# A list scheduler for the float32 items, the weight decoding and the first 20 steps of attention with two MLPs

## The chip, the cores and the metric

One core of a Trainium2 chip runs the kernel. The metric is the device time of one execution in microseconds (us). Engines: PE is TensorE, ACT is ScalarE, DVE is VectorE, POOL is GpSimd, SP is SyncE, whose queue issues the DMAs.

## The reference

Attention over a window of 128 keys for B = 4, H = 8, S = 576, D = 64, then two MLPs on the 2304 tokens of 512 features:

```python
scores = np.where(mask, scale * (q @ k.T) + bias, -1000000000.0)
attn = np.exp(scores - np.max(scores, axis=-1, keepdims=True))
attn = attn / (np.sum(attn, axis=-1, keepdims=True) + 1e-09)
x = (attn @ v).transpose(0, 2, 1, 3).reshape(2304, 512)
h = x @ w_in                                      # 512 -> 2048
x = (np.maximum(h, 0.0) + alpha * np.minimum(h, 0.0)) @ w_out
h = x @ w_in2
out = (h * (1.0 / (1.0 + np.exp(-1.702 * h)))) @ w_out2
```

The MLP weights come as float64.

## The kernel before

**Items.** An item is one head of one batch and one of two row ranges, 64 in all. The first `FP = 24` are done in float32 ahead of everything else; the others are interleaved with the later MLP steps. An item n of the first 24 goes through: `a_load` (two DMAs into one of five raw buffers: q and k at L412, v at L414), `a_qk` (PE, scores `s`), `a_bias` (DVE, L490), `a_exp` (ACT, L506), `a_sum` (POOL, an add on `st`, L521), `a_recip` (DVE, L516), `a_norm` (DVE, L537), `a_trans` (PE transposes, L552), `a_pt_hi` (ACT copies the transposed scores to `pt`, L559), `a_split_v` (POOL copies v from the raw buffer to a zero-padded `vz`, L448), `a_av` (PE, `o<-pt,vz`, L609), and after every second item `a_xf` (ACT and DVE split the result into `xh` and `xl`). `pt`, `tt` and `st` have three buffers, `vz` two. `busy(n)` puts idle matmuls between the first items. A raw buffer is loaded anew when its scores and its `vz` copy are done.

**Decoding.** The first MLP's weights are 32 chunks: chunk 2f is the `w_in` part and chunk 2f+1 the `w_out` part of block f. A chunk is loaded (`w_load`, 512 KB into one of four staging buffers `ws`), scaled twice on ACT (`w_scale`, `wd<-ws` and `ws<-ws`, L152, L155), shifted and added on DVE (`w_shift` L159, `w_add` L164), and split by `w_split` into `wh` (ACT) and `wl` (DVE), both through the helpers at L110 and L115. `wd` has three buffers.

**Steps.** Behind the items come steps (k, f). The first 32 alternate between two token blocks, k = 0, 1, with f = s // 2 for step s. `m1_h` makes h(s) with 12 matmuls (L680) from `xh`, `xl` and block f's `wh`, `wl`, in the order wh, wh, wl for each quarter; `m1_n` (ACT, L694) and `m1_g` (DVE L700, then ACT's cast `gh` L702) apply the slope of the first MLP; `m1_lo` (DVE) makes `gl`; `m1_o` adds g's product with the `w_out` part (12 matmuls, L726), `LAG = 2` steps later. PE's order is h(s), o(s-2), h(s+1), o(s-1), and so on.

**What sets the order.** All of it is written by hand. The item loop over n emits the stages of several items in a fixed pattern, a raw load for item n+4, and at the loop's steps named in `DEC` one pass of decoding. In the loop over steps each step up to s = 31 does one load (`w_ahead`), shift, add, split and scale through `w(...)`, which takes the next chunk for that stage. `chain(mark)` pins each engine's program order as written for the items; `pinned` and `held` do so for the steps. The minimum of the two halves of `relt` (a mask for later items, L1141) is written behind the items.

Of the kernel before, what the change touches and what calls it, by code (L numbers as in the profile page):

```python
# [11 lines left out]
F32 = mybir.dt.float32  # L12
# [9 lines left out]
P = 128  # L22
# [50 lines left out]
def tile_window_attention__then__two_mlps(  # L73
# [47 lines left out]
    def pin(ins):  # L121
        if pinned:
            tc.keep_in_program_order(ins)
# [22 lines left out]
        return s[:, :, 0], s[:, :, 1]  # L146

    def w_scale(i):
        lo, hi = w_words(i)
        layer, f, part = chunks[i]  # L150
        wtm[i] = wtmp.tile([P, DM], I32, tag="wd", name="wd")
        pin(nc.scalar.activation(  # L152
            wtm[i].bitcast(F32), hi.bitcast(F32), AF.Prelu, scale=2.0**-112, alpha=-(2.0**32)
        ))
        pin(nc.scalar.mul(lo, lo.bitcast(U32), 2.0**-29))  # L155

    def w_shift(i):
# [440 lines left out]
    @stage  # L598
    def a_av(n, b, u, h, U):
        if n < FP:  # L600
            if h % 2:
                x = st["x", n] = st["x", n - 1]
            else:
                i = n // 2 % 2
                x = pso.tile([P, 2, T1], F32, tag=f"o{i}", name=f"o{i}").rearrange("p i t -> p (i t)")
                st["x", n] = x
            pt, vz = pts[n % 3], vzs[n % 2]
# [488 lines left out]
    a_load(4, (0,))  # L1096
    a_load(3, (1,))
    bias_load(4, 4)
    make_identity(nc, ident)
    make_own()  # L1100
    busy(0)

    def only(fn, n, *args):
        if n < FP:
            fn(n, *args)

    for n in range(-1, FP + 4):
        only(a_qk, n + 1)
        busy(n + 2)
        only(a_bias, n)  # L1110
        only(a_xf, n - 4, 0)
        only(a_pt_hi, n - 2)
        only(a_av, n - 3)
        only(a_recip, n - 1)
        only(a_norm, n - 1, "dve")
        only(a_trans, n - 1)
        only(a_xf, n - 4, 1)
        only(a_exp, n)
        only(a_split_v, n - 1)
        only(a_sum, n)  # L1120
        if n == 0:
            a_load(4, (1,))
        elif 0 < n < FP - 4:
            a_load(n + 4)
        elif FP - 4 < n < FP - 1:
            a_load(n + 3)
        if n in (8, 10, 12, 14):
            w_load(wdone.setdefault("load", 0))
            wdone["load"] += 1
        if n == 16:  # L1130
            nc.sync.dma_start(out=relt, in_=rel)
            nc.sync.dma_start(out=alph, in_=alpha)
        if n in DEC:
            w("split")
            w("shift")
            w("add")
            w_ahead()
            w("scale")
    chain(mark)
    nc.gpsimd.tensor_scalar(beta, alph, -1.0, 1.0, op0=ALU.mult, op1=ALU.add)  # L1140
    nc.vector.tensor_tensor(relt[:, :P], relt[:, :P], relt[:, P:], op=ALU.min)  # L1141
    at0.close()
    pa.close()
    a_parts()
    pj = ExitStack()
    psa["j"] = pj.enter_context(tc.tile_pool(name="ps_j", bufs=1, space=PSUM))
    psa["a"] = pj.enter_context(tc.tile_pool(name="ps_b", bufs=2, space=PSUM))
    gp[0] = p1.enter_context(tc.tile_pool(name="g", bufs=3, side="right"))
    gt[0] = p1.enter_context(tc.tile_pool(name="gt", bufs=2, side="right"))
    xsp[0] = p1.enter_context(tc.tile_pool(name="xs", bufs=2, side="right"))  # L1150
# [316 lines left out]
```

## Time and profile before

| | us |
|---|---|
| median of 3 runs (lowest, highest) | 883.58 (882.83, 889.0) |
| the profiled execution | 884.44 |
| its span | 882.7 |
| PE busy in the span | 866.8 (98%) |
| DVE busy | 696.7 (79%) |
| ACT busy | 551.7 (62%) |
| POOL busy | 184.8 (21%) |

The items take the first 58.8 us (h(0) starts at 58.79), the 32 steps go on to about 145, and the rest of the span is later steps, the second MLP and the output. Rows of the trace are read as follows: a timeline row has its start, its length, the engine, the line, the operation, output <- inputs, and in brackets how long the engine was idle before it and what it waited for. A row of waits names the engine that waited, its instruction, and what ended the wait. The times between the starts of two rows of one engine tell what an operation costs in a row of others; its own length also has the part that overlaps.

### The profile page before, as it was taken

What the parts mean: (1) busy time and instruction counts of PE and PEld (TensorE: products, weight loads), DVE (VectorE), ACT (ScalarE), POOL (GpSimd) and SP (SyncE); (2) the same over time, 40 slices, a digit from 0 to 9 for tenths busy, and PEclk for the clock granted to TensorE, in tenths of its full rate; (3) what the DMA queues carried; (4) which work ended last, traced back from release to release, by engine and by line L of the source; (5) the groups of instructions that cost most, each with busy time, mean ns of one, the idle gap of its engine ahead of it and who ended that gap; (6) DMA issues with size and microseconds to landing.
All of it is one profiled execution on the core that took longest, in us unless ns stands there. A gap on an engine that the chain in (4) does not pass through costs nothing.

```text
span 882.7 us, 19445 instructions
## 1 busy us (share of the span) xinstructions
PE 866.8 (98%) x6804; PEld 838.2 (95%) x6804; DVE 696.7 (79%) x1763; ACT 551.7 (62%) x1397; POOL 184.8 (21%) x349
## 2 busy tenths in 40 slices
PE   9879999999999999999999999999999999999998
PEld 7769999999999999999988889999999999999997
DVE  5689887679999999999567777557575699988875
ACT  6798886677677767676455557655556754444432
POOL 3220002355666556655200000000000000000000
PEclk9999999999999999999999999999999999999999
DMA  4756662224335234242042334757678873544423
GB/s 137 198 163 212 194 193 88 89 87 149 114 88 185 77 117 133 90 141 83 1 143 96 96 106 163 225 206 241 219 261 284 294 264 112 171 140 124 152 61 96
DMA packets 74209, 132.28 MB, mean 150 GB/s; under 512 B 14336, under 2 KB 33792, under 8 KB 74112
## 3 DMA queue, kind: packets, MB, share of 16 engines
q1 hardware_dynamic: 74112, 131.05, 47.1%
q8 instruction: 53, 0.87, 0.4%
q14 instruction: 44, 0.36, 0.1%
HBM read 94.31 MB, written 36.70 MB: 148 GB/s over the span
## 4 chain that ended last, share of the span: by engine, by line
PE 60%; ACT 0%; DVE 0%; issue 0%; DVEq 0%; ACTq 0%
PE p L980 19%; PE p L883 14%; PE h L680 9%; PE h L883 6%; PE p L726 5%; PE o L726 4%; PE x L621 1%; PE s L471 1%; PE pt L545 0%; PE s L472 0%; ACT oh L110 0%; DVE ob L997 0%; ACT G L892 0%; DVE se L997 0%; DVE wd L997 0%
## 5 line engine op out<-in xcount | busy, mean ns | idle before, releaser
L680 PE MATMUL h<-xh,wh 128*128 128x256 f32 (+1 forms) x512 | 149.8, 293 | 0.4 <-DVE g L700 0.4
L680 PE MATMUL h<-xh,wl 128*128 128x256 f32 (+1 forms) x512 | 149.5, 292 | 0.0
L680 PE MATMUL h<-xl,wh 128*128 128x256 f32 (+1 forms) x512 | 149.5, 292 | 0.0
L980 PE MATMUL p<-wl,oh 128*128 128x256 f32 x504 | 136.2, 276 | 0.0
L980 PE MATMUL p<-wh,oh 128*128 128x256 f32 x504 | 135.0, 277 | 0.3 <-ACT oh L110 0.3
L980 PE MATMUL p<-wh,ol 128*128 128x256 f32 x504 | 131.0, 276 | 0.0
L726 PE MATMUL o<-gh,wh 128*128 128x256 f32 x448 | 127.6, 285 | 0.0
L726 PE MATMUL o<-gl,wh 128*128 128x256 f32 x448 | 124.0, 277 | 0.0
L726 PE MATMUL o<-gh,wl 128*128 128x256 f32 x448 | 123.8, 276 | 0.0
L680 PEld LDWEIGHTS h<-xh,wh 128*128 128x128 f32 x512 | 96.7, 189 | 3.3 <-DVE g L700 0.6
L680 PEld LDWEIGHTS h<-xh,wl 128*128 128x128 f32 x512 | 96.6, 189 | 2.9
L680 PEld LDWEIGHTS h<-xl,wh 128*128 128x128 f32 x512 | 96.7, 189 | 2.7
L1011 POOL TENSOR_TENSOR ob<-wd,se 128x256 f32<-128x256 f32 x1 | 0.7, 746 | 448.2 <-ACT se L1009 448.2
L980 PEld LDWEIGHTS p<-wl,oh 128*128 128x128 f32 x504 | 94.6, 188 | 0.0
L980 PEld LDWEIGHTS p<-wh,oh 128*128 128x128 f32 x504 | 93.7, 188 | 0.5 <-ACT oh L110 0.5
L980 PEld LDWEIGHTS p<-wh,ol 128*128 128x128 f32 x504 | 91.3, 188 | 0.0
L694 ACT ACTIVATE n<-h 128x256 f32<-128x256 f32 (+1 forms) x128 | 52.0, 406 | 53.6 <-PE h L680 52.9
L726 PEld LDWEIGHTS o<-gl,wh 128*128 128x128 f32 x448 | 84.3, 188 | 0.1
L726 PEld LDWEIGHTS o<-gh,wh 128*128 128x128 f32 x448 | 84.2, 188 | 0.1
L726 PEld LDWEIGHTS o<-gh,wl 128*128 128x128 f32 x448 | 84.1, 188 | 0.0
L702 ACT CAST gh<-g 128x256 fp32r<-128x256 f32 x112 | 45.2, 404 | 60.4 <-DVE g L700 60.2
L110 ACT CAST oh<-gs 128x1024 fp32r<-128x1024 f32 (+1 forms) x40 | 38.1, 964 | 62.9 <-issue 28.2
(182 smaller groups left out, 2460.9 us busy)
## 6 DMA issues: line engine op xcount, KB each, us to landing
g2d<-G SPq DMA_DIRECT2D x64, 288.0 KB, 3.2
ws<-in_w_in_dram SPq DMA_DIRECT2D x32, 512.0 KB, 3.7
ws<-in_w_out_dram SPq DMA_DIRECT2D x32, 512.0 KB, 4.0
gr<-g2d SPq DMA_DIRECT2D x32, 512.0 KB, 4.1
raw<-in_u_dram SPq DMA_DIRECT2D x32, 352.0 KB, 3.0
raw<-in_u_dram SPq DMA_DIRECT2D x32, 160.0 KB, 2.5
xr<-x2d SPq DMA_DIRECT2D x40, 128.0 KB, 2.6
wo2d<-wd SPq DMA_DIRECT2D x16, 256.0 KB, 2.7
```

Of the source, the lines that this page charges most:

```text
L110: return nc.scalar.copy(o, i)
L471: keep(nc.tensor.matmul(o[:, :n_], q, kh[:, ks : ks + n_], start=True, stop=False))
L621: keep(nc.tensor.matmul(x[:, oc : oc + nq], v, p[:, col : col + nq], start=(i == 0 and k == 0), stop=(i == len(js) - 1 and k == (j < 4)), ...
L680: keep(nc.tensor.matmul(ph, w[:, 0, c * P : (c + 1) * P], x[:, c, r : r + n], start=(c == 0 and i == 0), stop=(c == NC - 1 and i == 2),))
L694: nc.scalar.activation(n, ph, AF.Relu, scale=-1.0)
L702: nc.scalar.copy(gh, g)
L726: keep(nc.tensor.matmul(o, w[:, 1, c * P : (c + 1) * P], g, start=(first and (k == KM or c % 2 == 0) and i == 0), stop=(last and i == 2), ...
L883: tc.keep_in_program_order(nc.tensor.matmul(o, w[:, cc * P : (cc + 1) * P], x[:, h, cc, i, :], start=first and cc == 0 and k == 0, stop=la ...
L980: mm = nc.tensor.matmul(o[:, m, :], g[:, a, m * P : (m + 1) * P], w, start=(p == 0 and m == 0 and i == 0), stop=(p == NF // 2 - 1 and i == 2),
L1011: nc.gpsimd.tensor_tensor(c11, p1_, p2_, op=ALU.add)
```

## The change

A function `emission()` builds a list of all operations of the 24 items, of their loads, of the decoding of 32 chunks and of the steps, with their dependences, a duration for each kind and a delay between engines, and schedules them: PE has a fixed order, each other engine takes the operation that can start first, and among equals the one due first. The list is cut where o(17) starts; n, g, gh and gl of the first `SJ = 20` steps are kept, and pieces of decoding whose chunk number is below one that was done are appended. The kernel then writes its program in that order, and `chain(mark)` pins it. From step 20 on the old loop goes on. `w_scale`, `w_split` and `m1_g` are cut into pieces so that each can be placed by itself, `vz` has four buffers, and two loads of items 24 and 25 follow the list. The `min` on `relt` is written behind it (L1257 in the new file).

```diff
-DEC = (19, 21, 23, 24, 25, 26)
+SJ = 20
+XLAG = 3
...
+def emission():
+    seq = []
+    for n in range(-1, FP + XLAG + 1):
+        for k, i in (("s", n + 1), ("b", n + 2), ("x", n - XLAG), ("tr", n - 1)):
...
+            bias=(("s", i), ("tr", i - 3)), exp=(("bias", i),), add=(("exp", i),), recip=(("add", i),),
+            norm=(("recip", i),), pt=(("tr", i), ("x", i - 3)), vz=(("raw", i), ("x", i - 4)),
+            xh=(("x", i),), xl=(("xh", i),), raw=(("vz", i - 5), ("s", i - 5)),
+            ld=(("ad", i - NST), ("s", 8 + 2 * i)), sc1=(("ld", i), ("lo", i - NWD)), sc2=(("ld", i),), sh=(("sc1", i),),
+            ad=(("sh", i), ("sc2", i)), hi=(("ad", i),), lo=(("hi", i),), n=(("h", i), ("gl", i - 2), ("xl", FP - 1), ("xl", FP - 3)),
+            g=(("n", i),), gh=(("g", i), ("o", i - 3)), gl=(("gh", i),), b=(),
...
+    stop = next(t for t, _, z in out if z == ("o", SJ - 1 - LAG))
+    rows = ("n", "g", "gh", "gl")
+    out = [(t, p, z) for t, p, z in out if t <= stop or z[0] in rows and z[1] < SJ]
+    out = [x for x in out if not (x[2][0] in rows + ("h", "o") and x[2][1] >= SJ)]
+    done = {z for _, _, z in out}
+    out = sorted(out, key=lambda x: (x[0], x[1]))
+    out = [z for _, _, z in out]
+    for k in ("ld", "sc1", "sc2", "sh", "ad", "hi", "lo"):
+        last = max(i for q, i in done if q == k or {q, k} in ({"hi", "lo"}, {"sc1", "sc2"}))
+        out += [(k, i) for i in range(last + 1) if (k, i) not in done]
+    return out
...
+    vzf = [first.tile([P, 2, P], F32, name=f"vzf{i}") for i in range(2)]
+    vzs += vzf
-            nc.gpsimd.tensor_copy(vzs[n % 2][:, :, d0 : d0 + D], vr)
+            nc.gpsimd.tensor_copy(vzs[n % 4][:, :, d0 : d0 + D], vr)
...
-    for n in range(-1, FP + 4):
...
+    for k, i in emission():
+        if (k, i) == ("n", 0):
+            joint()
+        emit[k](i)
+        if (k, i) == ("raw", FP - 1):
+            nc.sync.dma_start(out=relt, in_=rel)
+            nc.sync.dma_start(out=alph, in_=alpha)
+    chain(mark)
+    pinned.append(True)
+    nc.vector.tensor_tensor(relt[:, :P], relt[:, :P], relt[:, P:], op=ALU.min)
...
+    a_load(FP)
+    a_load(FP + 1)
     for s, (k, f) in enumerate(steps):
+        if s < SJ:
+            continue
```

PE's order of operations is the same in both programs. On the other engines it moves; three places are shown, with the rows of the program in each engine's order.

**Place 1, DVE and ACT about step 21.** In the rows a `wl12` or `wh12` belongs to block 12 (steps 24 and 25); the numbers behind the underscore tell tiles apart. `h_1727` of the old program and `h_1706` of the new one are h(21). DVE before, from g(20) on:

```order
L700 SCALAR_TENSOR_TENSOR g_1701<-n_1698,beta_73,h_1683 128x256
L164 ISA wd_1668<-ws_1568,wd_1668 128x1024
L700 SCALAR_TENSOR_TENSOR g_1745<-n_1742,beta_73,h_1727 128x256
L115 TENSOR_TENSOR gl_1706<-g_1701,gh_1703 128x256
L115 TENSOR_TENSOR wl12_1709<-wd_1626,wh12_1708 128x512
L159 TENSOR_SCALAR wd_1712<-wd_1712 128x512
L164 ISA wd_1712<-ws_1610,wd_1712 128x1024
L115 TENSOR_TENSOR gl_1750<-g_1745,gh_1747 128x256
L115 TENSOR_TENSOR wl12_1709<-wd_1668,wh12_1708 128x512
```

DVE now, from g(21) on:

```order
L808 SCALAR_TENSOR_TENSOR g_1724<-n_1721,beta_73,h_1706 128x256
L262 ISA wd_1656<-ws_1603,wd_1656 128x1024
L207 TENSOR_TENSOR gl_1729<-g_1724,gh_1726 128x256
L207 TENSOR_TENSOR wl11_1732<-wd_1654,wh11_1731 128x512
L257 TENSOR_SCALAR wd_1658<-wd_1658 128x512
L808 SCALAR_TENSOR_TENSOR g_1768<-n_1765,beta_73,h_1750 128x256
L262 ISA wd_1658<-ws_1563,wd_1658 128x1024
L207 TENSOR_TENSOR gl_1773<-g_1768,gh_1770 128x256
L207 TENSOR_TENSOR wl11_1732<-wd_1656,wh11_1731 128x512
```

Behind g(21) the old program splits chunks 24 and 25 (block 12), the new one chunk 22 (block 11), which h(22) reads; the shift and add in between belong to later chunks. ACT before, from n(20) on:

```order
L694 ACTIVATE n_1698<-h_1683 128x256
L694 ACTIVATE n_1742<-h_1727 128x256
L702 CAST gh_1703<-g_1701 128x256
L110 CAST wh12_1708<-wd_1626 128x512
L152 ACTIVATE wd_1712<-ws_1610 128x512
L155 ACTIVATE ws_1610<-ws_1610 128x512
L702 CAST gh_1747<-g_1745 128x256
L110 CAST wh12_1708<-wd_1668 128x512
```

ACT now, from n(21) on:

```order
L802 ACTIVATE n_1721<-h_1706 128x256
L247 ACTIVATE wd_1658<-ws_1563 128x512
L253 ACTIVATE ws_1603<-ws_1603 128x512
L814 CAST gh_1726<-g_1724 128x256
L202 CAST wh11_1731<-wd_1654 128x512
L247 ACTIVATE wd_1691<-ws_1677 128x512
L253 ACTIVATE ws_1677<-ws_1677 128x512
L802 ACTIVATE n_1765<-h_1750 128x256
```

Both programs have two scalings between an n and a gh. In the old one the `wh` behind gh(20) is of chunk 24, in the new one the `wh` behind gh(21) is of chunk 22.

**Place 2, POOL at the first items.** `st` is the add behind the exponentials of items 0, 1, 2; `vz` and `vzf` are the copies of v. Before:

```order
L521 TENSOR_SCALAR st0_133<-st0_133 128x2
L448 COPY vz0_152<-raw0_131 128x2x64
L521 TENSOR_SCALAR st1_134<-st1_134 128x2
L448 COPY vz1_153<-raw1_132 128x2x64
L521 TENSOR_SCALAR st2_135<-st2_135 128x2
L448 COPY vz0_152<-rawf0_122 128x2x64
```

Now:

```order
L556 COPY vz0_154<-raw0_133 128x2x64
L556 COPY vz1_155<-raw1_134 128x2x64
L556 COPY vzf0_125<-rawf0_122 128x2x64
L556 COPY vzf1_126<-rawf1_123 128x2x64
L629 TENSOR_SCALAR st0_135<-st0_135 128x2
L629 TENSOR_SCALAR st1_136<-st1_136 128x2
```

Adds and copies alternated; now four copies stand ahead of the first add. On DVE in the same place the three passes of item 2's bias moved ahead of item 0's reciprocal.

**Place 3, DVE about step 27.** `g_1995` before and `g_1984` now are g(27); `q` belongs to item 24, `wl14` and `wd_1821` to chunk 28, which h(28) reads. Before:

```order
L700 SCALAR_TENSOR_TENSOR g_1995<-n_1993,beta_73,h_1980 128x256
L115 TENSOR_TENSOR gl_1962<-g_1957,gh_1959 128x256
L115 TENSOR_TENSOR wl15_1965<-wd_1882,wh15_1964 128x512
L115 TENSOR_TENSOR gl_1999<-g_1995,gh_1997 128x256
L115 TENSOR_TENSOR wl15_1965<-wd_1922,wh15_1964 128x512
L700 SCALAR_TENSOR_TENSOR g_2035<-n_2033,beta_73,h_2015 128x256
```

Now:

```order
L808 SCALAR_TENSOR_TENSOR g_1984<-n_1981,beta_73,h_1968 128x256
L262 ISA wd_1863<-ws_1849,wd_1863 128x1024
L544 SCALAR_TENSOR_TENSOR q_145<-raw0_133,q_145 64x256
L257 TENSOR_SCALAR wd_1821<-wd_1821 128x512
L207 TENSOR_TENSOR gl_1989<-g_1984,gh_1986 128x256
L262 ISA wd_1821<-ws_1805,wd_1821 128x1024
L207 TENSOR_TENSOR wl14_1992<-wd_1821,wh14_1991 128x512
```

The old program splits the last two chunks, 30 and 31, about g(27); the new one adds and splits chunk 28 there, and the add stands behind that of chunk 29, the `q` and gl.

## Rows read from the trace of the kernel before

**Rows 1.** Busy time by stretch: from:to, length, busy us (count) per engine, clock.
```profile
52.50:57.50 5.00, 2.31 (x13) 1.70 (x12) 4.30 (x11) 4.58 (x11) 0.68 (x2) 1.00 0.47 153
57.50:62.50 5.00, 4.87 (x26) 4.72 (x27) 3.93 (x9) 4.09 (x8) 0.58 (x6) 0.66 0.74 211
70.00:110.00 40.00, 40.00 (x355) 40.00 (x355) 36.20 (x76) 33.77 (x75) 0.00 (x0) 1.00 0.66 199
```

**Rows 2.** Waits of PE, 0 to 66 us: total, times, longest.
```profile
PE pt L552 <- DVE ttf L537: 3.0, 3, 2.0
PE s L462 <- DMA rawf<-in_u_dram: 1.7, 2, 0.8
...
PE pt L552 <- DVE tt L537: 1.1, 2, 0.8
PE s L462 <- DMA raw<-in_u_dram: 0.8, 1, 0.8
PE o L609 <- ACT ptf L559: 0.8, 1, 0.8
PE h L680 <- DVE g L700: 0.4, 1, 0.4
```

**Rows 3.** Waits of SyncE's queue, 0 to 60 us: total, times, longest.
```profile
SPq L414 <- POOL st L521: 13.3, 14, 2.3
```

**Rows 4.** Timeline, 41 to 42.6 us: start, length, engine, line, operation, [idle before <- releaser].
```profile
41.63 0.29 DVE L1141 TENSOR_TENSOR relt<-relt 128x128 f32<-128x128 f32 x1 [2.06 <-DMA relt<-in_rel_dram]
...
42.27 0.50 PE L552 MATMUL pt<-ident,ttf 128*128 128x128 f32 x2 [0.77 <-DVE ttf L537]
```

**Rows 5.** Timeline, 6.9 to 10 us.
```profile
6.99 0.58 SPq L414 DMA_DIRECT2D rawf<-in_u_dram  x1
...
8.11 0.22 POOL L521 TENSOR_SCALAR st<-st 128x2 f32<-128x2 f32 x1 [3.56 <-ACT tt L506]
...
8.61 0.16 DVE L516 RECIPROCAL st<-st 128x2 f32<-128x2 f32 x1
...
9.49 0.49 PE L552 MATMUL pt<-ident,tt 128*128 128x128 f32 x3
...
9.90 0.16 DVE L516 RECIPROCAL st<-st 128x2 f32<-128x2 f32 x1
```

**Rows 6.** DMA issues, 6.9 to 7.7 us: count, size each, median us to landing.
```profile
rawf<-in_u_dram SPq DMA_DIRECT2D x1, 64.0 KB, 2.5
```

**Rows 7.** Timeline of two steady steps, 119.5 to 125 us.
```profile
119.83 0.67 ACT L152 ACTIVATE wd<-ws 128x512 f32<-128x512 f32 x1
...
120.97 0.37 ACT L694 ACTIVATE n<-h 128x256 f32<-128x256 f32 x1
...
121.37 0.48 DVE L700 SCALAR_TENSOR_TENSOR g<-n,beta,h 128x256 f32<-128x256 f32 x1 [0.25 <-ACT n L694]
...
121.77 0.69 DVE L164 CUSTOM_DVE_ANT_0 wd<-ws,wd 128x1024 uint16<-128x1024 uint16 x1
...
121.89 0.41 ACT L702 CAST gh<-g 128x256 fp32r<-128x256 f32 x1 [0.55 <-DVE g L700]
121.95 0.28 PE L726 MATMUL o<-gh,wh 128*128 128x256 f32 x1
...
122.20 0.61 ACT L110 CAST wh<-wd 128x512 fp32r<-128x512 f32 x1
...
122.37 0.42 DVE L115 TENSOR_TENSOR gl<-g,gh 128x256 fp32r<-128x256 f32 x1
...
122.85 0.69 DVE L115 TENSOR_TENSOR wl<-wd,wh 128x512 fp32r<-128x512 f32 x1
...
123.31 0.28 PE L680 MATMUL h<-xh,wh 128*128 128x256 f32 x1
...
124.67 0.28 PE L726 MATMUL o<-gh,wh 128*128 128x256 f32 x1
...
124.93 0.39 ACT L694 ACTIVATE n<-h 128x256 f32<-128x256 f32 x1 [0.69 <-PE h L680]
```

More of the change, by code (lines that the diff above doesn't have):

```diff
@@ L58 @@
 WARM = (9, 3, 3, 2, 1, 1, 1)
+SJ = 20
+XLAG = 3
+ENGINES = dict(
+    PE=dict(s=0.66, tr=0.33, x=0.65, b=0.22, h=1.37, o=1.37),
+    DVE=dict(bias=0.6, recip=0.22, norm=0.5, xl=0.37, sh=0.44, ad=0.67, lo=0.67, g=0.43, gl=0.4),
+    ACT=dict(exp=0.98, pt=0.42, xh=0.31, sc1=0.63, sc2=0.63, hi=0.57, n=0.4, gh=0.37),
+    POOL=dict(vz=0.33, add=0.24),
+    SP=dict(raw=0.85, ld=2.3),
+)
+COST = {k: (e, c) for e, d in ENGINES.items() for k, c in d.items()}
+DELAY = dict(PE=0.28, DVE=0.12, ACT=0.15, POOL=0.2, SP=2.0)
@@ new lines, in emission, with needs, latest @@
+def emission():
+    seq = []
+    for n in range(-1, FP + XLAG + 1):
+        for k, i in (("s", n + 1), ("b", n + 2), ("x", n - XLAG), ("tr", n - 1)):
+            if 0 <= i < (len(WARM) if k == "b" else FP):
+                seq.append((k, i))
+    for i in range(2 * NF + LAG):
+        seq += [(k, j) for k, j in (("h", i), ("o", i - LAG)) if 0 <= j < 2 * NF]
+    place = {z: i for i, z in enumerate(seq)}
+    ops = set(seq)
+    for i in range(FP):
+        ops |= {(k, i) for k in ("bias", "exp", "add", "recip", "norm", "vz", "pt")}
+        ops |= {(k, i) for k in ("xh", "xl")[: 2 * (i % 2)]} | {("raw", i)} - {("raw", j) for j in range(5)}
+    for i in range(2 * NF):
+        ops |= {(k, i) for k in ("ld", "sc1", "sc2", "sh", "ad", "hi", "lo", "n", "g", "gh", "gl")}
+    banks = [("bias" if k == "s" else "pt", i) for k, i in seq if k in ("s", "tr")]
+    def needs(k, i):
+        if k in ("s", "tr"):
+            j = banks.index(("bias" if k == "s" else "pt", i))
+            return (("raw" if k == "s" else "norm", i),) + ((banks[j - 4],) if j > 3 else ())
+        return dict(
+            x=(("pt", i), ("vz", i), ("xl", i - 3)),
+            h=(("lo", i // 2 * 2), ("xl", 15 if i % 2 else 7), ("g", i - 2)),
+            o=(("lo", i // 2 * 2 + 1), ("gl", i), ("xl", FP - 1), ("xl", FP - 3)),
+            bias=(("s", i), ("tr", i - 3)), exp=(("bias", i),), add=(("exp", i),), recip=(("add", i),),
[4 more added lines that the diff above has]
+            g=(("n", i),), gh=(("g", i), ("o", i - 3)), gl=(("gh", i),), b=(),
+        )[k]
+    deps = {z: [y for y in needs(*z) if y in ops] for z in ops}
+    after = {z: [] for z in ops}
+    for z in ops:
+        for y in deps[z]:
+            after[y].append((z, DELAY[COST[y[0]][0]] if COST[y[0]][0] != COST[z[0]][0] else 0))
+    for y, z in zip(seq, seq[1:]):
+        after[y].append((z, 0))
+    due = {}
+    def latest(z):
+        stack = [z]
+        while stack:
+            y = stack[-1]
+            more = [x for x, _ in after[y] if x not in due]
+            if more:
+                stack += more
+            else:
+                due[y] = min([0.0] + [due[x] - d for x, d in after[y]]) - COST[y[0]][1]
+                stack.pop()
+    for z in ops:
+        latest(z)
+    wait = {e: sorted((z for z in ops if COST[z[0]][0] == e), key=lambda z: (place.get(z, 0), due[z], z)) for e in ENGINES}
+    free, end, out = dict.fromkeys(ENGINES, 0.0), {}, []
+    while any(wait.values()):
+        best = None
+        for e, l in wait.items():
+            for z in l[: 1 if e == "PE" else 40]:
+                if all(y in end for y in deps[z]):
+                    t = max([free[e]] + [end[y] + (DELAY[COST[y[0]][0]] if COST[y[0]][0] != e else 0) for y in deps[z]])
+                    if best is None or (round(t, 3), due[z], z) < best[0]:
+                        best = (round(t, 3), due[z], z), e, z, t
+        _, e, z, t = best
+        end[z] = free[e] = t + COST[z[0]][1]
+        wait[e].remove(z)
+        out.append((t, place.get(z, -1), z))
+    stop = next(t for t, _, z in out if z == ("o", SJ - 1 - LAG))
[9 more added lines that the diff above has]
+    return out
@@ L148, in w_scale, with w_scale_hi @@
     def w_scale(i):
+        w_scale_hi(i)
+        w_scale_lo(i)
+    def w_scale_hi(i):
         lo, hi = w_words(i)
[L150 removed]
         wtm[i] = wtmp.tile([P, DM], I32, tag="wd", name="wd")
@@ L176, in w_split, with w_split_hi @@
             return
+        w_split_hi(i)
+        w_split_lo(i)
+    def w_split_hi(i):
+        layer, f, part = chunks[i]
         if part == 0:
@@ L1101, in tile_window_attention__then__two_mlps @@
     busy(0)
-    def only(fn, n, *args):
-        if n < FP:
-            fn(n, *args)
-    for n in range(-1, FP + 4):
[L1108 to L1150, printed above, removed]
     steps = [(k, f) for f in range(NF) for k in range(2)]
@@ L1153, in tile_window_attention__then__two_mlps, with joint, piece, run @@
     S2 = 2 * NF
+    pj = ExitStack()
+    def joint():
+        nc.gpsimd.tensor_scalar(beta, alph, -1.0, 1.0, op0=ALU.mult, op1=ALU.add)
+        at0.close()
+        pa.close()
+        a_parts()
+        psa["j"] = pj.enter_context(tc.tile_pool(name="ps_j", bufs=1, space=PSUM))
+        psa["a"] = pj.enter_context(tc.tile_pool(name="ps_b", bufs=2, space=PSUM))
+        gp[0] = p1.enter_context(tc.tile_pool(name="g", bufs=3, side="right"))
+        gt[0] = p1.enter_context(tc.tile_pool(name="gt", bufs=2, side="right"))
+        xsp[0] = p1.enter_context(tc.tile_pool(name="xs", bufs=2, side="right"))
+    def piece(name, fn):
+        def run(i):
+            fn(i)
+            wdone[name] = max(i + 1, wdone.get(name, 0))
+        return run
+    emit = dict(
+        s=a_qk, b=busy, x=a_av, tr=a_trans, bias=a_bias, exp=a_exp, add=a_sum, recip=a_recip,
+        norm=lambda n: a_norm(n, "dve"), vz=a_split_v, pt=a_pt_hi, xh=lambda n: a_xf(n, 0), xl=lambda n: a_xf(n, 1),
+        raw=a_load, ld=piece("load", w_load), sc1=w_scale_hi, sc2=piece("scale", w_scale_lo), sh=piece("shift", w_shift),
+        ad=piece("add", w_add), hi=w_split_hi, lo=piece("split", w_split_lo),
+    )
+    emit |= {k: lambda i, f=f: f(*steps[i]) for k, f in dict(h=m1_h, n=m1_n, g=m1_g, gh=m1_gh, o=m1_o).items()}
+    emit["gl"] = lambda i: m1_lo(*steps[i], "dve")
+    pinned.clear()
+    for k, i in emission():
[8 more added lines that the diff above has]
+    nc.vector.tensor_tensor(relt[:, :P], relt[:, :P], relt[:, P:], op=ALU.min)
     def item_t(o):
```

17 lines of the change are left out of this document (13 added, 4 removed).

## The prediction

> **What bounds the kernel now.** First the busy time by stretch [rows 1]: TensorE (PE) is busy for all of 70 to 110 us, so it bounds the kernel there, and it was busy for only 2.31 of the 5 us before 57.5. Only time in which PE waits ahead of the two-block steps can be won. Next PE's waits from 0 to 66 us [rows 2]: 3.0 + 1.1 us on the normalised scores (`ttf`, `tt`), 1.7 + 0.8 on raw loads, 0.8 on `ptf`, 0.4 on the first `g`, together 7.8 us (waits for the warm-up's operand, ahead of the work, are left out). Third, the clock: behind the half idle 5 us the granted clock was 0.66 for 5 us [rows 1], for a part of them the 1.2 GHz level. That costs 5 x 0.34 = 1.7 us. All that the front of the program can give back is 7.8 + 1.7 = 9.5 us, 1.1% of the run.
>
> **What goes.** The raw loads are late because SyncE, waiting at L414 for a GpSimd instruction, holds up its queue for 13.3 us in 14 waits [rows 3]: the copy `vz` has to be done before a raw buffer is free, and with two `vz` buffers it waits for the value product of two items back. Four buffers move that wait two items further back, so I take the 2.5 us as gone. The waits for `tt`, `ttf` and `ptf`, 4.9 us, come from decoding that is written between the items; the list puts the items' own work first. One stays: the `min` on `relt` stood 2.06 us in VectorE's queue for its load, with the norm of an item behind it, and PE paid 0.77 [rows 4]. In the new order it stands between the reciprocal and the norm of item 19, and its load is issued behind the last raw load. So 4.9 - 0.8 = 4.1 goes. The 0.4 for the first `g` is a latency (h(0), n, g, h(2)) that no order shortens. If PE has no half idle 5 us ahead of h(0), the 1.7 us of low clock go too. Sum: 2.5 + 4.1 + 1.7 = 8.3 us.
>
> **What the new order adds at the start.** GpSimd now copies four `vz` before its first `add` (place 2 of the change). The fourth waits for the second half of `rawf1`, issued at 6.99 us [rows 5]; such loads land 2.5 us after issue [rows 6], here at 9.5. With a few tenths for the copy the first `add` starts near 9.9 in place of 8.11. Behind it come at most 0.5 us to the reciprocal (8.11 to 8.61) and 0.88 to the first transpose (8.61 to 9.49), so 11.2 at most in place of 9.49. VectorE alone now does the third bias pass ahead of the first reciprocal; that pass was over at 9.90 [rows 5], which with 0.88 gives 10.8. So the loss is between 1.3 and 1.7 us, and less where a later item makes some of it up; I take 1.4, and 0.5 to 2.0 as its ends. A cast of item 24's keys stands on ScalarE ahead of the exponential of item 22 and waits for a late load. The nearest row is the `relt` wait: 0 to 0.8 for PE, of which I take 0.2, since PE runs two items behind that exponential. Net gain of the front: 8.3 - 1.4 - 0.2 = 6.7 us.
>
> The Trainium skill ("PSUM — Partial Sum Buffer", section "Engine vs sequencer instructions") says that the queues of ScalarE, VectorE and GpSimd are strict FIFO; the trace agrees, by the 2.06 us for which a norm stood behind the `min` [rows 4]. Were a ready instruction let past a waiting one, the 1.4 us at the start and most of the loss in the next part would not arise; by the rule they do.
>
> **What the new order does to decoding, where I expect the loss.** A weight chunk is decoded by two ScalarE scalings, a shift and an add on VectorE, the `wh` cast on ScalarE and the `wl` subtraction on VectorE. Step s has a product h(s), then n, g, gh, gl, and o(s) on PE two steps later. h(s) of an even step takes chunk s: its first matmul reads `wh`, its third `wl`. In the old order `wl` of chunk s stands on VectorE behind g of step s-4 or s-3 from step 4 on. The scheduler's list ends with step 19 and leaves chunks split only up to 20; from there one chunk a step is split, as before. So `wl` of chunk s stands behind g(s-1) (place 1), and h(22), h(24), h(26), h(28) and h(30) each wait for a chain that begins only when h(s-1) ends. Odd steps read weights that the even one waited for, and an odd chunk is first read by o(s), two steps later.
>
> The chain with durations of the steady stretch [rows 7], from T = end of h(s-1). n starts at T + 0.26 (124.93, where the o behind h starts at 124.67). ScalarE then has two scalings of another chunk: 0.28 behind n's start, 1.14 for both (119.83 to 120.97), so gh starts at T + 1.68, though g would allow T + 1.2 (0.40 from n to g, 0.52 from g to gh). `wh` starts 0.31 behind gh (121.89, 122.20), T + 1.99, `wl` 0.65 behind `wh` (122.85), T + 2.64; it takes 0.69, to T + 3.33, and PE goes on at T + 3.4. Undisturbed, PE does an o first, 1.36 us (121.95 to 123.31), and the third matmul of h(s) follows 2/12 of 1.36 later, at T + 1.6. So 1.8 us are lost. For the five steps:
> - h(24), h(26): the first scaling waits for `wl` of the odd chunk as well, 0.1: 1.9 each.
> - h(22): VectorE's add for chunk 23 waits for the second scaling, T + 1.85; 0.6 for the add and 0.42 for gl (121.77, 122.37) put `wl` at T + 2.87: 2.0.
> - h(28): VectorE has g, an add, a `q` step of item 24, a shift, gl and only then the add of chunk 28 itself (place 3). `q` waits for ScalarE's `q`, which stands behind the scalings, to about T + 2.2. With three operations of about 0.4 the add starts at 3.3 and ends at 3.9, and `wh` and `wl` follow, 0.65 + 0.69: T + 5.3, a loss of 3.7.
> - h(30): item 24's reductions and norm stand ahead of g(29), some 1.5 us more; gh and `wh` are then no longer behind the scalings, 0.5 less: about 2.7.
> Sum 2.0 + 1.9 + 1.9 + 3.7 + 2.7 = 12.2 us. Bounds: 1.8 for each, 9.0, and 14 if nothing overlaps in the last two. Behind step 31 the order is the old one, and PE, busy for all of a steady stretch [rows 1], has no slack in which to make it up.
>
> **Sum.** Against the profiled run of 884.4 us (its span is 882.7): 884.4 - 6.7 + 12.2 = 889.9. The median of the runs is 0.9 us lower, so 889.0 us, 0.6% slower. A measurement of this kernel can tell about 1% from no change; the bounds are 874.7 and 892.4.
>
> **Rivals.**
> 1. The late splits cost nothing, since ScalarE and VectorE run so far ahead that `wl` is ready when h(s) comes. For it: VectorE was busy for 36.20 of 40 us [rows 1] with all of the decoding in it, so it can keep pace. Against it: the chain begins at h(s-1) itself, and keeping pace does not shorten it. The time is 883.6 - 6.7 = 876.9, faster than before; with the whole 8.3 us it is 875.3, and with 9.5 874.1, faster by over 1%. If half of the loss comes, 883.
> 2. The front does not do what it says: the list rests on durations written into the kernel, and in a fixed order one late load on SyncE or ScalarE holds up the items behind it, as SyncE's queue was held for 13.3 us [rows 3]. If the 4.1 us for `tt`, `ttf` and `ptf` come back at other items, the front gains 2.6 and the time is 883.6 - 2.6 + 12.2 = 893.2. It decides, slower by over 1%, where the front gains less than 3.4 us.
> 3. The clock falls between steps 28 and 31, where PE waits 3.7 + 2.7 us beside four steps of 2.72 (121.95 to 124.67 is one): busy for 10.9 of 17.3 us, 0.63, against 2.31 of 5, 0.46, ahead of the old fall [rows 1]. One fall costs about 1.7 us, 890.7; two, 892.4, slower by 1%. Against it: 0.63 is well above 0.46.
> The Trainium skill ("TensorE: Matmul & The Clock Gate", section "Part 1: The HAM clock gate") says that the throttled clock is the default and activity releases it; the fall behind the half idle 5 us agrees [rows 1]. By it each of the five waits could bring a fall, and the sum would be as in rival 3.
>
> **How the numbers follow.** The forecast (front 4 to 8, loss 9 to 14) has 0.62 and a range of its own from 885 to 893.5; rival 1 has 0.14, half of it over 1%; rival 2 0.14; rival 3 0.10. The range of all goes down into the half loss and rival 1, to 879, and up past rivals 2 and 3, to 896. Faster by over 1%: 0.07. Slower: rival 2 with 0.14, 0.04 of rival 3 and 0.04 of the forecast's top end, 0.22. Within 1%: 0.71.
>
> **What would show it.** In the new trace: no PE wait on raw loads ahead of h(0); the first transpose near 10.9 us; h(0) and h(1) at full clock; no wait from h(3) to h(21); then five waits of h on ScalarE's `wh` and VectorE's `wl` in every second step, of 1.8 to 3.7 us, the largest at the first step with item 24. It is wrong if those five are missing, or if the front keeps waits of over 4 us.

## The result, and the profile after

| | before | changed |
|---|---|---|
| median of 14 runs, us | 885.44 (882.83 to 889.0) | 890.97 (887.9 to 893.69) |
| ratio | | 1.0064, 95% interval 1.0049 to 1.0078 |
| profiled execution, us (span) | 884.44 (882.7) | 887.9 (886.1) |

The changed kernel is 0.6% slower; 889.0 against a median of 883.6, 1.0061, had been predicted. The two profiled executions differ by 3.5 us, and what follows explains these; the medians differ by 2 us more, to which the last section returns.

The busy time by stretch of the changed kernel, with the columns of [rows 1]:

```profile
52.50:57.50 5.00, 4.66 (x41) 4.46 (x40) 4.97 (x11) 4.69 (x11) 0.39 (x1) 1.00 0.43 146
57.50:62.50 5.00, 5.00 (x46) 5.00 (x46) 4.97 (x11) 4.35 (x11) 0.00 (x0) 1.00 0.66 210
70.00:110.00 40.00, 39.51 (x349) 39.31 (x347) 33.92 (x72) 33.96 (x74) 0.00 (x0) 1.00 0.62 195
110.00:130.00 20.00, 16.56 (x130) 15.55 (x131) 12.77 (x26) 12.80 (x27) 0.00 (x0) 1.00 0.46 135
130.00:135.00 5.00, 2.04 (x18) 1.84 (x16) 3.65 (x9) 2.72 (x6) 0.00 (x0) 1.00 0.34 102
135.00:140.00 5.00, 4.78 (x27) 4.57 (x27) 2.84 (x10) 3.47 (x11) 0.74 (x1) 0.66 0.38 111
```

The 5 us before 57.5 are busy now, the clock stays at 1.00 there, and the steady stretch is reached earlier. But from 110 on PE is busy for 16.56 of 20 us, then for 2.04 of 5, and behind that the granted clock is 0.66 for 5 us. PE's waits from 0 to 66 us, as [rows 2] (the warm-up's row left out):

```profile
PE pt L660 <- POOL st L629: 1.5, 1, 1.5
...
PE h L788 <- DVE g L808: 0.3, 1, 0.3
PE o L717 <- DVE st L624: 0.3, 1, 0.3
```

Of the 7.8 us of [rows 2] 0.3 is left, for g; new are 1.5 us for GpSimd's add and 0.3 for a reciprocal (`st`). PE's waits from 66 to 170 us, where the kernel before has only 1.6 us on the last of these rows:

```profile
PE h L788 <- ACT wh L202: 7.2, 5, 3.0
PE h L788 <- DVE wl L207: 1.2, 5, 0.3
PE x L729 <- issue: 0.8, 1, 0.8
```

Five waits each for `wh` and `wl`, at h(22), h(24), h(26), h(28) and h(30). The chain ahead of h(22), in the timeline, can be laid beside the walk of the prediction:

```profile
107.98 0.28 PE L838 MATMUL o<-gh,wh 128*128 128x256 f32 x1
...
108.24 0.39 ACT L802 ACTIVATE n<-h 128x256 f32<-128x256 f32 x1 [0.92 <-PE h L788]
...
108.53 0.67 ACT L247 ACTIVATE wd<-ws 128x512 f32<-128x512 f32 x1
...
109.62 0.41 ACT L814 CAST gh<-g 128x256 fp32r<-128x256 f32 x1
...
109.91 0.64 ACT L202 CAST wh<-wd 128x512 fp32r<-128x512 f32 x1
...
110.71 0.68 DVE L207 TENSOR_TENSOR wl<-wd,wh 128x512 fp32r<-128x512 f32 x1
...
111.45 0.38 PE L788 MATMUL h<-xh,wl 128*128 128x256 f32 x1 [0.35 <-DVE wl L207]
```

h(21) ends where the o begins, T = 107.98. n comes at T + 0.26, gh behind the scalings at T + 1.64 (1.68 foreseen), `wh` at T + 1.93, `wl` at T + 2.73, and PE goes on with the third matmul at T + 3.47. Ahead of h(28):

```profile
130.24 0.28 PE L838 MATMUL o<-gh,wh 128*128 128x256 f32 x1
...
132.28 0.42 DVE L544 SCALAR_TENSOR_TENSOR q<-raw,q 64x256 fp32r<-64x256 f32 x1 [0.34 <-ACT q L542]
...
133.39 0.68 DVE L262 CUSTOM_DVE_ANT_0 wd<-ws,wd 128x1024 uint16<-128x1024 uint16 x1
134.11 0.62 ACT L202 CAST wh<-wd 128x512 fp32r<-128x512 f32 x1 [1.57 <-DVE wd L262]
...
135.50 0.39 PE L788 MATMUL h<-xh,wl 128*128 128x256 f32 x1 [0.22 <-DVE wl L207]
```

T is 130.24. `q` comes at T + 2.0 (2.2 foreseen), the add of chunk 28 at T + 3.2 (3.3), `wh` at T + 3.9 (3.9), and PE's third matmul at T + 5.3 (5.3).

The starts of h(s), less those of the kernel before, in each profiled execution (from the timelines; h(19) to h(21) are alike where nothing is said):

| | h(0) | h(3) | h(21) | h(23) | h(25) | h(27) | h(29) | h(31) | behind the first items of the steps |
|---|---|---|---|---|---|---|---|---|---|
| changed | -7.28 | -8.53 | -8.53 | -6.44 | -4.56 | -2.64 | 2.77 | 4.52 | 3.6 |
| e1 late decoding, old order | -1.69 | -1.16 | 0.35 | 1.97 | 3.46 | 5.09 | 6.59 | 10.73 | 10.65 |
| e2 list to step 26 | -5.05 | -6.29 | -6.29 | -6.29 | -6.29 | -6.29 | -4.27 | -2.70 | -2.57 |
| e3 old order, four vz | -1.10 | -1.19 | -1.20 | -1.20 | -1.19 | -1.19 | -1.20 | -1.20 | -1.23 |
| e4 start | -7.21 | -8.43 | -8.44 | -6.43 | -4.59 | -2.76 | 1.07 | 5.04 | 4.52 |
| e5 fill | -7.41 | -8.55 | -6.63 | -4.58 | -2.74 | -0.91 | 2.92 | 5.22 | 7.50 |
| e7 start and min | -8.78 | -10.01 | -10.01 | -7.93 | -6.06 | -4.14 | 0.94 | 4.80 | 4.39 |
| e9 list to step 28 | -6.36 | -7.73 | -5.81 | -5.60 | -5.39 | -5.17 | -5.00 | -5.00 | -2.53 |
| e10 the same, start and min | -8.82 | -10.27 | -10.27 | -10.27 | -10.27 | -10.27 | -10.26 | -10.27 | -10.18 |
| e11 list with two vz | -1.70 | -2.86 | -2.86 | -2.86 | -2.86 | -2.86 | -2.86 | -2.86 | -2.69 |

In the changed kernel 8.53 us are won by h(3), nothing changes up to h(21), 13.05 are lost from there to h(31), and 0.9 come back later: 3.6, the difference of the spans (3.4) but for 0.2.

### The profile page after: what moved, and what is told of

Same layout as the page of the kernel before. It is cut to its first block, busy times and chain, and to the rows that moved or that the text cites. A ratio compares the mean times of both kernels' runs of the same rounds, so it can differ in the third digit from the quotient of the medians.

```text
span 886.1 us, 19432 instructions
## 1 busy us (share of the span) xinstructions
PE 868.0 (98%) x6803; PEld 838.6 (95%) x6804; DVE 696.5 (79%) x1763; ACT 551.3 (62%) x1397; POOL 186.5 (21%) x351
## 4 chain that ended last, share of the span: by engine, by line
PE 60%; ACT 0%; DVE 0%; issue 0%; DVEq 0%; ACTq 0%
PE p L1092 19%; PE p L995 14%; PE h L788 9%; PE h L995 6%; PE p L838 5%; PE o L838 4%; PE x L729 1%; PE s L579 1%; PE pt L653 0%; PE s L580 0%; ACT oh L202 0%; DVE ob L1109 0%; ACT G L1004 0%; DVE se L1109 0%; DVE wd L1109 0%
```

## The experiments

**e1: the loss without the change.** The kernel before, with the decoding passes of three steps dropped: the same chunks are decoded, but later.

```diff
+        dec = s < S2 and s not in (16, 17, 18)
-        if s < S2:
+        if dec:
             w_ahead()
...
```

> The kernel before, with its decoding pass left out in steps 16, 17 and 18, so that wl of a chunk stands one step ahead of its use from step 20 on, as in the changed kernel; the front is as before and no work is taken away. Theory (the lead alone makes the loss): waits of h on wh and wl in the steps 20 to 30, 1.9 us each for four, and 1.8 to 5.4 us for h(28) and 1.8 to 2.7 for h(30): 11 to 15 us over before, a ratio of 1.012 to 1.017. Rival (the loss comes from the scheduler's first 20 steps, which leave VectorE or ScalarE behind): within 2 us of before.

Ratio 1.0098, interval 1.0069 to 1.0128; 894.22 us. PE's waits from 66 to 170 us:

```profile
PE h L680 <- ACT wh L110: 5.1, 6, 1.8
...
PE h L680 <- DVE wl L115: 1.3, 6, 0.2
```

Six waits, at every even step from h(20) on; between h(19) and h(31) 11.9 us are lost, 1.5 to 1.6 a step and 4.1 at h(30), where the clock fell (granted clock 0.66 from 150 to 155 us). The lead alone makes the loss, as the theory has it. The steps cost 0.3 us less than the 1.9 that I had said. The ratio stands for 8.7 us, below the 11 to 15 that had been expected; 1.2 us of the difference were won by h(3) in this execution, where nothing had been changed.

**e2: the list carried on to step 26.**

```diff
-SJ = 20
+SJ = 26
```

> The changed kernel with the list carried on to step 26 in place of 20. Theory (a boundary effect of the cut): the waits at h(22), h(24) and h(26) go, 5.9 us; those at h(28) and h(30) stay, with or without the fall of the clock: ratio to before 0.995 to 1.001. Rival (the front's gain was taken out of the time for decoding, and VectorE cannot keep pace with one chunk a step): the waits stay where they are or come in other steps, ratio 1.003 to 1.008.

Ratio 0.995, interval 0.9931 to 0.997; 880.42 us. PE's waits from 66 to 170 us:

```profile
PE h L788 <- ACT wh L202: 1.9, 2, 1.1
...
PE h L788 <- DVE wl L207: 0.6, 2, 0.4
```

The waits at h(22), h(24) and h(26) are gone and two are left, 2.0 us for h(28) and 1.6 for h(30) by the table. Up to chunk 26 `wl` of an even chunk stands on VectorE behind g of two or three steps before, and it is done 0.7 to 1.3 steps ahead of its use from step 8 on, so VectorE keeps pace. So the loss is no matter of throughput; it lies in the cut of the list, behind which the loop over steps splits one chunk a step, each one step ahead of its use. The front gains 2.2 us less here than in the changed kernel, though up to the cut its list is the same: PE waits 2.7 us for the first add in this execution, in place of 1.5, and the granted clock is 0.66 from 10 to 15 us.

**e3: four vz buffers in the kernel before.**

```diff
-            nc.gpsimd.tensor_copy(vzs[n % 2][:, :, d0 : d0 + D], vr)
+            nc.gpsimd.tensor_copy(vzs[n % 4][:, :, d0 : d0 + D], vr)
...
```

> The kernel before with four vz buffers and nothing else. Theory: the three waits of PE for raw loads go, 2.5 us by the table of waits and up to 3.0 with PE's restarts: ratio 0.9963 to 0.9975. Rival: the loads come earlier, but the items behind them wait for VectorE at the same places, less than 1 us: ratio 0.999 to 1.000.

Ratio 0.9991, interval 0.9966 to 1.0016. PE's waits from 0 to 66 us:

```profile
PE pt L554 <- DVE ttf L539: 2.9, 3, 1.7
PE pt L554 <- DVE tt L539: 2.4, 2, 1.7
PE s L464 <- DMA rawf<-in_u_dram: 1.3, 2, 0.9
...
PE s L464 <- DMA raw<-in_u_dram: 0.6, 1, 0.6
```

SyncE's waits from 0 to 60 us:

```profile
SPq L141 <- DVE wd L164: 13.6, 5, 5.7
...
SPq L416 <- POOL st L523: 3.8, 5, 1.9
SPq L416 <- POOL vzf L450: 2.5, 5, 0.8
...
SPq L416 <- POOL vz L450: 1.0, 1, 1.0
```

SyncE stands 7.3 us for GpSimd at that line in place of 13.3 [rows 3], but PE still waits 1.9 us for raw loads in place of 2.5, and 5.3 us for `tt` and `ttf` in place of 4.1. Between 20 and 42 us, where weights are loaded too, the 64 KB loads now take a median of 4.4 and 4.3 us to land (3.5 and 3.2 in the kernel before), and at the weight loads (L141) SyncE now stands 13.6 us for VectorE's add in place of 9.6, with the raw loads behind in its queue. Either can eat up an earlier issue; which of the two does is not shown. The rival holds: the buffers alone win 1.2 us by h(3).

**e4: the start.** Two more dependences in the list of the changed kernel.

```diff
-            bias=(("s", i), ("tr", i - 3)),
+            bias=(("s", i), ("tr", i - 3)) + ((("norm", 0),) if i == 2 else ()),
-            vz=(("raw", i), ("x", i - 4)),
+            vz=(("raw", i), ("x", i - 4)) + ((("add", 0),) if i == 3 else ()),
```

> The changed kernel with two more dependences in the list: the fourth vz behind the first add, and item 2's bias behind item 0's norm. Theory (both queues hold the first transpose up): first transpose at 9.5 to 9.8 us in place of 11.11, and all behind it 1.3 to 1.6 us earlier, since PE is busy from 20 to 40 us: ratio to before 1.004 to 1.005 where the changed kernel has 1.0064. Rival (a later item makes it up): the first transpose is earlier, h(0) is not.

Ratio 1.004, interval 1.0023 to 1.0057. The first transpose:

```profile
9.83 0.49 PE L660 MATMUL pt<-ident,tt 128*128 128x128 f32 x3
```

In the changed kernel this is

```profile
11.11 0.61 PE L660 MATMUL pt<-ident,tt 128*128 128x128 f32 x3 [1.49 <-POOL st L629]
```

The start is 1.3 us earlier, and h(0) is where it was (51.58 against 51.51). It is given back at one place:

```profile
43.32 0.61 PE L660 MATMUL pt<-ident,tt 128*128 128x128 f32 x3 [1.09 <-DVE tt L645]
```

The `min` waits for `relt` until 42.69, and PE for the norm behind it. Here it is:

```profile
42.69 0.29 DVE L1257 TENSOR_TENSOR relt<-relt 128x128 f32<-128x128 f32 x1 [1.63 <-DMA relt<-in_rel_dram]
```

and in the changed kernel:

```profile
42.62 0.29 DVE L1257 TENSOR_TENSOR relt<-relt 128x128 f32<-128x128 f32 x1 [0.57 <-DMA relt<-in_rel_dram]
```

In the changed kernel it goes at 42.62, after a wait of 0.57 that PE does not feel. So the rival holds in these two executions (the ratio, 1.004, is in the theory's range, but its interval overlaps that of the changed kernel, 1.0049 to 1.0078, so the medians do not decide it), and the late start and the `min` are not two losses but one: the load of `relt` is a floor for the front.

e4 shows one thing more, since its clock is still full ahead of h(30), where it had fallen in the changed kernel. h(29) ends at T = 139.90 in e4; g(29) and the third matmul of h(30) follow:

```profile
141.84 0.47 DVE L808 SCALAR_TENSOR_TENSOR g<-n,beta,h 128x256 f32<-128x256 f32 x1
...
144.05 0.58 PE L788 MATMUL h<-xh,wl 128*128 128x256 f32 x1 [0.21 <-DVE wl L207]
```

In the changed kernel T is 141.55:

```profile
142.73 0.47 DVE L808 SCALAR_TENSOR_TENSOR g<-n,beta,h 128x256 f32<-128x256 f32 x1
...
144.94 0.39 PE L788 MATMUL h<-xh,wl 128*128 128x256 f32 x1 [0.23 <-DVE wl L207]
```

The matmul comes at T + 4.2 in e4 and at T + 3.4 in the changed kernel; undisturbed it would be at T + 1.6, so that 2.6 and 1.8 us are lost. From g(28) to g(29) VectorE has 4.6 us of work in e4 and 4.8 in the changed kernel, item 24's with it. PE ends h(29) 2.7 us behind the start of g(28) in e4, and 3.6 us behind it in the changed kernel, where the o between them runs at the low clock. So VectorE is less far behind there, and a part of what the fall costs comes back. In e7 the clock had fallen too, but was full again at that o: PE takes 2.8 us there, and the matmul comes at T + 4.1.

**e5: PE kept busy ahead of h(28).** The changed kernel with 24 matmuls whose result is not used.

```diff
+        if s == S2 - 4:
+            fill = psa["a"].tile([P, 512], F32, tag="a", name="fill")
+            for _ in range(24):
+                keep(nc.tensor.matmul(fill[:, :T1], wt[0, 0][0][:, 0, :P], xh[:, 0, :T1], start=True, stop=True))
```

> The changed kernel with 24 matmuls more, about 2.7 us, whose result nobody reads, put on PE ahead of h(28), where PE waits 3.0 us. Theory (the longest wait is what lets the clock fall, and that costs 1.7 us of the 5.4 between h(27) and h(29)): granted clock 1.00 from 130 to 145 us, loss at h(28) 3.7 us, the end 1.0 to 1.7 us earlier than in the changed kernel. Rival (the low clock in the rows costs no time, or the wait has nothing to do with it): loss at h(28) 5.4 or more, the end the same or later.

Ratio 1.0069, interval 1.0048 to 1.009. Busy time from 130 to 140 us:

```profile
130.00:135.00 5.00, 5.00 (x47) 5.00 (x46) 3.85 (x9) 3.04 (x7) 0.00 (x0) 1.00 0.09 11
135.00:140.00 5.00, 4.46 (x37) 4.06 (x36) 2.69 (x7) 3.03 (x7) 0.46 (x1) 1.00 0.55 202
```

The clock stays at 1.00, and from h(27) to h(29) 3.83 us are lost in place of 5.41: the fall costs 1.6 us there, as the theory has it. The end isn't earlier, against the theory: this execution lost 1.9 us between h(3) and h(21), where no wait is (the last section says how), and 2.3 more behind the steps, where PE waits 2.3 us for ScalarE in place of 1.6 in the kernel before and the clock falls behind that wait (0.75 from 160 to 165 us).

**e6 and e8: a first form of the list to step 28**, without and with the edits of e7. In both the load of item 24 stands ahead of item 20's reads of the same buffer, so that item 20 is computed from item 24's data; the amount of work is the same.

```diff
-SJ = 20
+SJ = 28
...
+        if (k, i) == ("gl", 25):
+            a_split(FP)
         if (k, i) == ("raw", FP - 1):
             nc.sync.dma_start(out=relt, in_=rel)
             nc.sync.dma_start(out=alph, in_=alpha)
+            a_load(FP)
...
-    a_load(FP)
```

> The changed kernel with the list carried on to step 28, the split of item 24's q and k put behind gl(25) in it, and item 24's load behind the loads of relt and alph. Theory (boundary of the cut): no wait on wh or wl at h(22) to h(28), at most 1.0 us at h(30), PE all busy from 60 to 130 us; ratio to before 0.988 to 0.993. Rival (VectorE cannot keep three chunks ahead to the end): waits of 2 us or more between h(22) and h(30), ratio over 0.995.

> All three together: list to step 28, the two dependences at the start, the min behind g(2). If the theories of the other three hold, the gains add: ratio to before 0.986 to 0.991, about 1.3 us less than the list to step 28 alone. Rival: the start is given back elsewhere, and the time is that of the list to step 28 alone.

Ratios 0.9919 (0.9901 to 0.9936) and 0.9915 (0.9897 to 0.9932). Neither has a wait for `wh` or `wl`. The gains do not add in the medians: e8 is above its range and no faster than e6. e9 and e10 are the same with the load in its place.

**e7: the start and the min.** e4, with the `min` written behind g(2) in the list.

```diff
+        if (k, i) == ("g", 2):
+            nc.vector.tensor_tensor(relt[:, :P], relt[:, :P], relt[:, P:], op=ALU.min)
...
-    nc.vector.tensor_tensor(relt[:, :P], relt[:, :P], relt[:, P:], op=ALU.min)
```

> The changed kernel with the two dependences of the run on the start, and the min on relt pinned behind g(2). Theory (what is won at the start is given back at the min, which waits for its load until 42.7 us whatever stands ahead of it): no wait of PE near 43 us, h(0) at 50.0 to 50.6 us in place of 51.5, ratio to before 1.002 to 1.004. Rival (raw loads or decoding give it back as well): h(0) within 0.4 us of 51.5.

Ratio 1.0048, interval 1.0029 to 1.0066. PE does not wait near 43 us, and h(0) starts at 50.01: the theory of the front holds, 1.5 us are won there, but the ratio is above its range. What was won is lost again at h(28) and h(30), 5.1 and 3.9 us, where the clock fell both times (granted 0.83 from 130 to 140 us, 0.85 and 0.81 in the next two stretches of 5 us).

**e9 and e10: the list to step 28**, with item 24's load behind g(0); e10 with the edits of e7. The edit is shown against e6.

```diff
+        if (k, i) == ("g", 0):
+            a_load(FP)
         if (k, i) == ("raw", FP - 1):
             nc.sync.dma_start(out=relt, in_=rel)
             nc.sync.dma_start(out=alph, in_=alpha)
-            a_load(FP)
```

> The list carried on to step 28, with item 24's load behind g(0) in the list, so that it cannot stand ahead of item 20's reads of the same buffer. Theory (boundary of the cut): no wait on wh or wl from h(22) to h(30) over 0.3 us, h(3) 7 to 8.5 us earlier than before, ratio to before 0.989 to 0.993. Rival (VectorE cannot keep chunks three steps ahead to the end): waits of 2 us or more, ratio over 0.995.

> The same with the two dependences at the start and the min on relt behind g(2). Theory (the run on relt showed h(0) at 50.0): 1.0 to 1.5 us less than the list to step 28 alone, ratio 0.987 to 0.991. Rival (the start is given back elsewhere, or PE's pace in the steps differs from execution to execution by more than that): no difference that the intervals show.

e9: 877.31 us, ratio 0.9923 (0.9899 to 0.9947). e10: 877.08 us, ratio 0.9921 (0.9897 to 0.9945). There is no wait for `wh` or `wl` in either, and both are faster than both kernels. In the profiled execution of e10 the front is 10.27 us ahead of the kernel before and stays so. The two medians do not differ, as the rival of e10 has it, and e10's ratio is above its range.

**e11: the list with two vz buffers.**

```diff
-            vz=(("raw", i), ("x", i - 4)),
+            vz=(("raw", i), ("x", i - 2)),
-            nc.gpsimd.tensor_copy(vzs[n % 4][:, :, d0 : d0 + D], vr)
+            nc.gpsimd.tensor_copy(vzs[n % 2][:, :, d0 : d0 + D], vr)
...
```

> The changed kernel with two vz buffers in place of four, in the list's dependences and in the kernel; the list then puts more decoding ahead of h(0), and wl of every chunk four steps or more ahead of its use. Theory (the loss in steps 22 to 30 is a matter of the lead alone, and the four buffers are what lets the raw loads come in time): no wait on wh or wl in the steps, waits for raw loads of 1.5 to 2.5 us ahead of h(0), h(3) 2.5 to 5 us earlier than before, ratio 0.993 to 0.998. Rival (four buffers matter little in the list's order too): h(3) over 6 us earlier, ratio below 0.993.

Ratio 0.9997, interval 0.9974 to 1.0019. No wait for `wh` or `wl`; of PE's waits from 0 to 66 us those for raw loads are back:

```profile
PE s L570 <- DMA rawf<-in_u_dram: 1.8, 3, 0.9
...
PE s L570 <- DMA raw<-in_u_dram: 0.8, 1, 0.8
```

h(3) is 2.86 us earlier than before, as the theory has it; the ratio is above what was expected, and the profiled execution loses nearly 6 us behind the steps (last section); why the median shows nothing of the 2.9 us is not shown. The list alone gives 2.9 us, the buffers alone 1.2 (e3), both together 8.5. The three do not decode alike, though: ahead of h(0) five chunks are split here, one in the changed kernel and three in the kernel before. So part of the 8.5 us is decoding put off into the steps, and how much the buffers give by themselves in the list's order is not separated from it.

## Why the prediction was right, by its steps

- **What bounds the kernel.** Right. Up to h(31) all of the difference between the two profiled executions lies at steps where PE waits, or where the clock is low behind a wait.
- **What goes: 8.3 us of the 9.5 that could.** Too small: with the later start, 8.5 + 1.6 = 10.1 us went. All waits of [rows 2] but that for g are gone, 7.5 us, and the 1.7 of low clock. The 0.8 kept for the `min` did not come, since PE is later there (e4). What is left, 0.9 us, is in no row of waits; a wait ends in its row where the first instruction starts, and what PE needs to be at its pace again is not in it. That reading is argued, not tried. The waits for the norms went in part because decoding was put off: one chunk is split ahead of h(0), where it had been three. The 0.2 for the cast of item 24's keys did not come, since ScalarE does not wait for its load.
- **Why the raw loads were late.** Half right. SyncE's wait for `vz` was there, but e3 shows that four buffers alone take away 0.6 of the 2.5 us. With the list and two buffers they stay, 2.6 us (e11). For these waits it takes both.
- **The start, 1.4 us.** 1.62, within the ends given. It cost nothing in the sum, because the `min` would have cost as much (e4); both out of the way are worth 1.5 us (e7). Both are an instruction held up by the one ahead of it in its engine's queue: PE waited 1.49 us for the add behind four copies, and 1.09 us (e4) for the norm behind the `min`. The Trainium skill ("PSUM — Partial Sum Buffer", section "Engine vs sequencer instructions") says that the queues of these engines are strict FIFO, and the runs agree.
- **The loss in steps 22 to 30, 12.2 us.** 13.05 us, from the cause named: e1 makes it without the change, e2 and e9 take it away. By steps, with full clock where a run shows it: h(22) 2.1 (2.0 foreseen), h(24) 1.9 (1.9), h(26) 1.9 (1.9), h(28) 3.8 (3.7; e4 and e5, 5.4 with the fall of the clock). h(30) lost 1.75 where 2.7 had been foreseen, because the clock had fallen ahead of it: with full clock up to there it lost 2.6 (e4), and 0.8 of the 1.6 us of the fall came back. At full clock the five steps make 12.3 us, where the sum was 12.2; the fall, given as a rival with 1.7 us, adds 0.8.
- **Behind the steps** I saw nothing; 0.9 us came back, most of it at a wait of PE behind step 31 that took 1.6 us before and 0.8 now. It took 0.8 to 2.3 us in the other runs.
- **The sum** of -8.5 + 13.05 - 0.9 is 3.6 us where -6.7 + 12.2 gave 5.5. The front was worth 1.8 us more; the fall of the clock (0.8) and what came back behind the steps (0.9) nearly cancel. That the measured ratio is nevertheless the predicted one is in part luck: it owes 2 us to what the medians differ by beyond the two profiled executions. Some of that seems to be further falls of the clock, rival 3, to which 0.10 had been given; the rest is open (last section).

## What to carry to other kernels

A list of instructions that is cut somewhere must be judged by the state it leaves: here every chunk was ready in time up to the cut, and behind it a loop that does one chunk a step kept for ever the lead of one step that it was handed. Busy shares do not show this (VectorE was busy for 33.92 of 40 us while it kept two to three ahead); the order of an instruction and of what it is for does, since a wait whose chain begins at the step before has a length that can be added up from the rows. And a gain in front of a late load ends at that load: look for the floor before the gain is counted.

## What the runs showed of the hardware that was not expected

In the steady stretch PE has two paces at a granted clock of 1.00. Busy time with counts of matmuls, from 80 to 100 and from 720 to 770 us, of the kernel before:

```profile
80.00:100.00 20.00, 20.00 (x179) 20.00 (x178) 17.67 (x37) 16.73 (x37) 0.00 (x0) 1.00 0.68 197
720.00:770.00 50.00, 50.00 (x444) 50.00 (x443) 47.94 (x96) 23.62 (x38) 0.00 (x0) 1.00 0.54 166
```

of e9:

```profile
80.00:100.00 20.00, 20.00 (x172) 20.00 (x171) 17.88 (x38) 17.17 (x38) 0.00 (x0) 1.00 0.64 211
720.00:770.00 50.00, 50.00 (x444) 50.00 (x443) 47.91 (x95) 24.00 (x38) 0.00 (x0) 1.00 0.50 150
```

and of e10:

```profile
80.00:100.00 20.00, 20.00 (x178) 20.00 (x178) 18.05 (x39) 17.70 (x39) 0.00 (x0) 1.00 0.71 219
720.00:770.00 50.00, 50.00 (x427) 50.00 (x426) 45.73 (x91) 22.16 (x35) 0.00 (x0) 1.00 0.43 127
```

179 or 178 matmuls against 172 in 20 us, 444 or so against 427 in 50 us, with no wait in either: 4% apart. e9 had the longer pace in the steps and not at the end, e10 the other way round. A step of 24 matmuls takes 2.72 or 2.83 us; e5, e8 and e9 had the longer pace from h(3) on. e5 lost it behind its first wait. For e8 and e9 the difference ends at step 28, where item 24's matmuls come in and the kernel before goes over to 2.83 us a step itself, so the pace changes inside an execution too. Over the 25 steps from h(3) to h(28) that is 2.7 us, and from 715 us to the end 6, in e10 as in e11. It differs between executions of one kernel as it seems (e10's six runs go from 874.72 to 880.42 us), so that a profiled execution alone can hide a gain of 6 us. What sets it, no run here was made to tell.

The clock did not fall at the same wait each time. In e4:

```profile
130.00:135.00 5.00, 1.97 (x17) 1.70 (x15) 3.74 (x9) 2.73 (x6) 0.00 (x0) 1.00 0.35 107
135.00:140.00 5.00, 4.78 (x41) 4.65 (x40) 3.31 (x12) 4.23 (x12) 0.75 (x1) 1.00 0.32 107
140.00:145.00 5.00, 2.94 (x19) 2.52 (x18) 3.88 (x9) 1.31 (x3) 0.88 (x1) 0.88 0.60 170
145.00:150.00 5.00, 5.00 (x37) 5.00 (x36) 2.30 (x9) 2.48 (x9) 1.94 (x5) 0.78 0.01 2
```

PE was busy for 1.97 of 5 us ahead of h(28) and the clock held, where it fell behind 2.04 of 5 in the changed kernel; here it fell behind 142 us. In e7 it fell at both places. Laid beside the same step at full clock, a fall cost 1.3 to 1.6 us (1.6 by e5).

The record has the mean granted clock of every run, and a fall of the traces lowers it by 0.002. The changed kernel's profiled execution, with one fall, has 0.998, as has one more of its 14 runs (890.85 us); eight have 0.996 or 0.997 (889.1 to 891.64 us) and four 0.994 (892.21 to 893.69 us). The profile of e7, with two falls, has 0.996, so most runs of the changed kernel seem to pay for more than one. On average the mean is 0.9958 in the changed kernel and 0.9966 in the 52 runs of the kernel before that were timed beside the experiments, where both profiled executions have 0.998. The difference of 0.0008 is 0.7 us of clock, an estimate from these means: about a third of the 2 us by which the medians differ more than the profiled executions. The rest is open.
